# Attention scores from one product with the tokens on the partitions, and maxima and sums of phi taken by halves

## The chip, the cores and the metric

The kernel runs on one core of a Trainium2 chip. The metric is the device time of one execution in microseconds; the time of a version is the median of its runs. A profile is taken by the hardware profiler in one further execution, whose own time stands beside its rows.

Engines are named as the profile names them: PE (matrix products; PEld is its loading of weights, the operand that stays in the array), DVE (vector engine), ACT (scalar engine), POOL, and SP, which here issues DMAs. Each engine works through its own instructions strictly in the order in which they stand in the program.

## The reference

Three parts follow each other; the output of each feeds the next.

```python
# attention: q, k, v [8 batches, 8 heads, 576 tokens, 64], phi [8, 8, 576, 32]
a = exp(phi - phi.max(axis=tokens)); a = a / (a.sum(axis=tokens) + 1e-9)
k_m, v_m = a^T k, a^T v                     # 32 memory rows for each head
scores = (1/8) * q @ k_m^T                  # 576 x 32
attn = softmax(scores over the 32)
x = attn @ v_m                              # [4608 tokens, 512]
# mlp
x = relu(x @ w_in)**2 @ w_out               # 512 -> 2048 -> 512
# experts, top 1 of 8
e = argmax(x @ w_gate); g = softmax(x @ w_gate)[e]
out = g * (relu(x @ w1[e]) @ w2[e])         # 512 -> 1024 -> 512
```

`w_in` and `w_out` arrive as 64-bit floats and are converted on the chip.

## The kernel before

**Stages.** First a start-up, in which `w_in` and `w_out` are loaded in 32 pieces and converted (`conv`: one ACT and three DVE instructions each) and the attention of batch 0 is worked out. Then a main loop over 192 steps: 12 blocks of 384 tokens times 16 pieces of the 2048 hidden columns. Step n makes `h` by six products on PE (`g1`, line 650), three ACT instructions and one DVE instruction make the two halves of `g` from it (658, 660, 661, 662), and three steps later `g2` (line 670) makes nine products of 512 columns into three accumulators. `g` has four buffers. Last come the experts, some 39 tiles of 128 tokens, with weights fetched by expert.

**How attention enters.** The product with `w_in` is folded into the memory rows: for each batch `U = v_m w_in` (`u_steps`, lines 554 and 563 on PE, 569 on ACT, 570 on DVE, eight pieces of 512 columns), and `h` is `U` times the transposed softmax `attnT`. So `g1` of the first step that holds tokens of batch b has to wait for batch b's `attnT` and `U`. Those steps are 16 for batch 1, 32 + 16 = 48 for batch 2, 64 for batch 3, then 96, 112, 144 and 160.

**What one batch's attention does.** `attention(b)` is a generator; the main loop takes a step of it now and then (`R0`, `R1`, `R2` are steps per loop step, `due` and `rel` bound them). Its parts: the maximum of phi (336) over the six tokens j that one partition holds, then over the partitions on POOL, subtraction (343), exponential, the sum over j (350); `s_kv(g)` for two groups g of four heads: the products with phi's weights (366, 374); `s_tr`: their transposes and the block-diagonal `kb` and `vbd`; `s_q`: the transposed queries `qT` of a pair of heads; `s_sc(g)`: scores with the memory rows on the partitions (453), copied by ACT to `sT` (459); `s_soft(g)`: transposes of `sT` back to tokens on partitions (469), then the softmax on DVE and ACT; `s_back(g)`: transposes (492) into `attnT` (496, 497). A phi tile, `e_t`, has one buffer: batch b+1 is loaded when batch b's products have read it.

**Beside it.** `weight_stream` reads the experts' weights through four staging tiles, takes their squares (601, ACT) or maxima (180, DVE), splits them in two halves (628 ACT, 629 DVE) and writes them back. `route` takes each finished block's rows: copies from the accumulators (`x2f`, 706 and 708), scaling into `rec` (723, 724), logits, and a scatter by POOL into a table; the small copy of token numbers into `rec` (791) for the next block has to wait until the scatter of this block has read `rec`.

**What sets the order.** The kernel is recorded in the order of the code, and a scheduler then places the instructions of each engine by its own estimate of when each can run, with priorities around the attention's steps. So an edit moves much more than the lines that it touches. Tiles of the `sd` tag are PSUM banks, three in all, which the attention, `u`, logits and ranks share.

Of the kernel before, what the change touches and what calls it, by code (L numbers as in the profile page):

```python
# [12 lines left out]
F32 = mybir.dt.float32  # L13
# [3 lines left out]
AF = mybir.ActivationFunctionType  # L17
ALU = mybir.AluOpType
AX = mybir.AxisListType
# [4 lines left out]
P = 128  # L24
B, H, S, D, M = 8, 8, 576, 64, 32
DM, DFF, NT, E, F = 512, 2048, 4608, 8, 1024
PS, NJ = 96, 6
# [32 lines left out]
def tile_attention__then__moe__then__moe2(  # L60
# [14 lines left out]
    V, A, G, T, SP = nc.vector, nc.scalar, nc.gpsimd, nc.tensor, nc.sync  # L75
# [5 lines left out]
    ps = ctx_side.enter_context(tc.tile_pool(name="ps", bufs=1, side="right"))  # L81
# [17 lines left out]
    def side_bank(name):  # L99
        return pp.tile([P, 512], F32, tag="sd", name=name, bufs=3)  # L100
# [5 lines left out]
    ident = const([P, P], F32, "ident")  # L106
# [223 lines left out]

    def attention(b):
# [3 lines left out]
        with tc.issue_after(late[b]) if b in late else ExitStack():  # L335
            V.tensor_reduce(
                mx.rearrange("p (h m) -> p h m", h=H), e_t[:PS].rearrange("p h j m -> p h m j"),
                axis=AX.X, op=ALU.max,
            )
# [10 lines left out]
        V.tensor_reduce(  # L350
            es.rearrange("p (h m) -> p h m", h=H), e_t.rearrange("p h j m -> p h m j"),
            axis=AX.X, op=ALU.add,
        )
# [91 lines left out]
        sT, pt = {}, {}  # L445

        def s_sc(g):
            s = ps.tile([P, S], F32, tag="sT", name=f"sT{b}_{g}", bufs=1)
            sT[g] = s
            for hf in range(2):  # L450
                bank = side_bank(f"sc{b}_{g}_{hf}")
                for x in range(2):
                    T.matmul(
                        bank[64 * x:64 * x + 64, 0:288],
                        kbd[g][:, 64 * x:64 * x + 64],
                        qTs[2 * g + x][:, hf * 288:(hf + 1) * 288],
                        start=True, stop=True,
                    )
                A.activation(s[:, hf * 288:(hf + 1) * 288], bank[:, 0:288], AF.Copy)

        def s_soft(g):
# [3 lines left out]
            for hf in range(2):  # L465
                bank = side_bank(f"st{b}_{g}_{hf}")
                for j in range(3):
                    jj = 3 * hf + j
                    T.transpose(
                        bank[:PS, j * P:(j + 1) * P], sT[g][:, jj * PS:(jj + 1) * PS], ident  # L470
                    )
# [42 lines left out]
        s_sc(0)  # L514
# [5 lines left out]
        s_soft(0)  # L520
        yield
# [4 lines left out]
        yield  # L526
        s_sc(1)
# [701 lines left out]
```

## Time and profile before

| | |
|---|---|
| median of 3 runs | 1335.16 us (1334.47 to 1335.77) |
| profiled execution | 1334.69 us, span 1332.6 us |
| PE busy | 1173.5 us, 88% of the span |
| DVE busy | 676.7 us, 51% |
| ACT busy | 661.2 us, 50% |
| granted TensorE clock, mean | 0.958 |
| main loop, first `h` to the last accumulators | about 100 to 866 us |

Shares of busy time are means over stages: the experts keep DVE and ACT nearly idle, while in the main loop all three engines work close together. A busy PE is a union of modelled durations, so short gaps between products don't show in it. The granted clock is 1.00 or 0.50 at a time; a mean between them says how much of a stretch ran at either.

### The profile page before, as it was taken

How to read it: one execution, taken by the hardware profiler on the slowest of the kernel's cores; microseconds unless marked ns; L12 is line 12 of the kernel's file. 1: busy time of each engine (PE TensorE's matmuls, PEld its weight loads, DVE VectorE, ACT ScalarE, POOL GpSimd, SP SyncE). 2: the span in 40 equal slices, each digit the busy share in tenths (PEclk: the TensorE clock that was granted, in tenths of full speed). 3: DMA queues.
4: the chain of work that ended last, by engine and by line, in shares of the span. 5: the costliest groups of instructions: out<-in, count | busy, mean ns of one | idle time of the engine just before them, and what ended most of it. 6: DMA issues, size and time to landing. Idle time of an engine off the chain costs nothing.

```text
span 1332.6 us, 21300 instructions
## 1 busy us (share of the span) xinstructions
PE 1173.5 (88%) x7146; PEld 597.4 (45%) x7146; DVE 676.7 (51%) x1644; ACT 661.2 (50%) x1347; POOL 113.9 (9%) x169
## 2 busy tenths in 40 slices
PE   1538989998988998898999999998998998879896
PEld 1214546444545544455555465543443443334342
DVE  5798987877886885786546543342110111101100
ACT  2467877797875877685666665521111111111111
POOL 2000000101010101000000100013000000000000
PEclk9558999998989999898999999999999999999998
DMA  6957659468749469536040110476558457695762
GB/s 168 261 190 207 189 137 265 158 213 260 216 163 266 154 213 287 159 132 150 24 103 10 40 25 24 126 169 167 97 120 181 104 123 193 151 227 118 151 159 61
DMA packets 264369, 205.23 MB, mean 154 GB/s; under 512 B 209855, under 2 KB 228287, under 8 KB 264256
## 3 DMA queue, kind: packets, MB, share of 16 engines
q1 hardware_dynamic: 257616, 182.67, 53.7%
q0 software_dynamic: 6640, 21.16, 4.6%
q8 instruction: 58, 0.95, 0.3%
q14 instruction: 55, 0.45, 0.1%
HBM read 234.53 MB, written 55.76 MB: 218 GB/s over the span
## 4 chain that ended last, share of the span: by engine, by line
issue 33%; PE 24%; DMA 17%; DVE 13%; ACT 6%; POOL 4%; SPq 2%; POOLq 0%; ACTq 0%; DVEq 0%
PE acc L670 12%; DMA wstage<-in_moe_w_dram 6%; PE h L650 6%; POOL out_dram L92 3%; DMA scr<-rec,sl 2%; DMA e_t<-in_phi_dram 2%; DVE wo L629 2%; ACT wo L628 1%; DMA ws<-wo 1%; PE u L563 1%; DMA raw_ring<-in_moe_w_out_dram 1%; DVE g L662 1%; DMA raw_ring<-in_moe_w_in_dram 1%; ACT wo L601 1%; DVE wm L180 1%
## 5 line engine op out<-in xcount | busy, mean ns | idle before, releaser
L670 PE MATMUL acc<-wo,g 128*128 128x512 f16 x1728 | 421.1, 383 | 16.5 <-DVE g L662 9.9
L670 PEld LDWEIGHTS <-g 128*128 128x128 f16 x1728 | 166.0, 99 | 197.5 <-issue 22.1
L650 PE MATMUL h<-attnT,U 128*128 128x384 f16 (+1 forms) x1536 | 233.5, 290 | 13.8 <-ACT U L569 9.8
L1001 PE MATMUL e<-w2t,gT 128*128 128x512 f16 x936 | 211.5, 381 | 22.3 <-DMA gT<-g 14.6
L974 PE MATMUL e<-w1t,xT 128*128 128x512 f16 x936 | 211.2, 381 | 11.4 <-DMA w1t<-ws 8.0
L986 DVE SCALAR_TENSOR_TENSOR g<-e,g 128x512 f16<-128x512 f32 x78 | 50.3, 686 | 297.5 <-ACT g L985 297.3
L650 PEld LDWEIGHTS <-U 128*128 128x128 f16 x1536 | 140.1, 99 | 104.2 <-issue 26.6
L1001 PEld LDWEIGHTS <-gT 128*128 128x128 f16 x936 | 91.2, 98 | 137.4 <-DMA gT<-g 18.5
L974 PEld LDWEIGHTS <-xT 128*128 128x128 f16 x936 | 91.5, 98 | 124.9 <-issue 13.7
L662 DVE TENSOR_TENSOR g<-r,g 128x384 f16<-128x384 f32 x192 | 105.6, 553 | 78.3 <-ACT r L661 77.8
L658 ACT ACTIVATE r<-h 128x384 f32<-128x384 f32 x192 | 92.6, 485 | 80.7 <-PE h L650 58.7
L985 ACT ACTIVATE g<-e 128x512 f16<-128x512 f32 x78 | 42.3, 594 | 173.6 <-PE e L974 173.6
L1014 ACT ACTIVATE y<-e,fac 128x512 f32<-128x512 f32 x39 | 26.8, 688 | 197.9 <-PE e L1001 190.8
L660 ACT ACTIVATE g<-r 128x384 f16<-128x384 f32 x192 | 99.6, 522 | 8.8 <-PE acc L670 5.2
L661 ACT ACTIVATE r<-r 128x384 f32<-128x384 f32 x192 | 99.5, 521 | 3.9
L629 DVE SCALAR_TENSOR_TENSOR wo<-wstage,wsc,wo 128x1024 f16<-128x1024 f32 x64 | 81.1, 1280 | 21.7 <-ACT wo L628 21.6
L628 ACT ACTIVATE wo<-wstage,wsc 128x1024 f16<-128x1024 f32 x64 | 71.7, 1144 | 25.0 <-DMA ws<-wo 12.6
L92 POOL DMA_INDIRECT out_dram<-y,rt x39 | 37.9, 972 | 377.1 <-ACT y L1014 356.5
L92 POOL DMA_INDIRECT scr<-rec,sl x36 | 37.6, 1043 | 301.8 <-DVE sl L788 66.7
L366 PE MATMUL kvm<-kv,e_t 128*32 128x128 f32 x768 | 28.0, 302 | 28.4 <-ACT e_t L348 27.4
L180 DVE TENSOR_REDUCE wm<-wstage 128x1 f32<-128x1024 f32 x32 | 38.8, 1214 | 14.4 <-DMA wstage<-in_moe_w_dram 14.3
L601 ACT ACTIVATE wo<-wstage 128x1024 bf16<-128x1024 f32 x32 | 33.7, 1054 | 12.3 <-DMA wstage<-in_moe_w_dram 11.0
(240 smaller groups left out, 1088.2 us busy)
## 6 DMA issues: line engine op xcount, KB each, us to landing
w1t<-ws SPq DMA_DIRECT2D x144, 512.0 KB
w2t<-ws SPq DMA_DIRECT2D x144, 512.0 KB
wstage<-in_moe_w_dram SPq DMA_DIRECT2D x64, 512.0 KB
ws<-wo SPq DMA_DIRECT2D x64, 512.0 KB
kv<-in_k_dram SPq DMA_DIRECT2D x16, 576.0 KB
kv<-in_v_dram SPq DMA_DIRECT2D x16, 576.0 KB
q<-in_q_dram SPq DMA_DIRECT2D x64, 144.0 KB
raw_ring<-in_moe_w_in_dram SPq DMA_DIRECT2D x16, 512.0 KB
```

Of the source, the lines that this page charges most:

```text
L92: i = G.indirect_dma_start(out=dst[:, :], out_offset=bass.IndirectOffsetOnAxis(ap=index, axis=0), in_=src, in_offset=None, bounds_check=bo ...
L180: V.tensor_reduce(dst, src, axis=AX.X, op=ALU.max, apply_absolute_value=True)
L628: A.activation(hi, src, AF.Copy, scale=s)
L629: V.scalar_tensor_tensor(lo, src, s, hi, ALU.mult, ALU.subtract)
L650: T.matmul(bank[:, off:off + w], u_t[b][:, g, uh, f * P:(f + 1) * P], attnT[b][:, g, ah, s0:s0 + w], start=(x == 0), stop=(x == len(seq) - 1),
L658: A.activation(r, bank[:, 0:BLK], AF.Relu, scale=2.0 ** -10)
L660: A.activation(g[:, 0], r, AF.Square)
L661: A.activation(r, r, AF.Square)
L662: V.tensor_tensor(g[:, 1], r, g[:, 0], op=ALU.subtract)
L670: T.matmul(a, g[:, gh, tt * P:(tt + 1) * P], wo[:, f, wh, :], start=(f == 0 and x == 0), stop=(f == NF - 1 and x == 2),)
L974: T.matmul(bank[hf], x[:, 4 * xh + c, :].bitcast(F16), w[c][:, wh * F + hf * 512:wh * F + (hf + 1) * 512], start=(c == 0 and xh == 0 and w ...
L1001: T.matmul(a, gT[:, 8 * gh + f, :], w[f // 2][:, o:o + DM], start=(f == 0 and x == 0), stop=(f == 7 and x == 2),)
```

## The change

There are two edits.

The maximum and the sum over the six tokens j of a partition were each one reduction over 1536 elements with stride. They become three elementwise instructions (`over_j`): of two pairs of j into a tile `oj` of 512 elements, with the last pair, and of its two halves into 256.

The scores were made with the memory rows on the partitions, copied to SBUF, and transposed back. Now the transposed queries are the weights and `kb` the moving operand, so that one product gives scores with the tokens on the partitions, in the bank from which the softmax reads. `s_sc`, `sT`, its copies and the transposes of `sT` go. The steps of the generator change with it: `s_soft(0)` stands where `s_sc(0)` stood, and `s_sc(1)`'s step is gone, so that a batch has two steps less.

```diff
+    def over_j(dst, src, op, name):
+        n = src.shape[0]
+        t = ps.tile([P, H, 2, M], F32, tag="oj", name=f"oj{name}", bufs=1)
+        V.tensor_tensor(t[:n], src[:, :, 0:2], src[:, :, 2:4], op=op)
+        V.tensor_tensor(t[:n], t[:n], src[:, :, 4:6], op=op)
+        V.tensor_tensor(dst.rearrange("p (h m) -> p h m", h=H), t[:n, :, 0], t[:n, :, 1], op=op)
...
-            V.tensor_reduce(
-                mx.rearrange("p (h m) -> p h m", h=H), e_t[:PS].rearrange("p h j m -> p h m j"),
-                axis=AX.X, op=ALU.max,
-            )
+            over_j(mx, e_t[:PS], ALU.max, f"mx{b}")
...
-        V.tensor_reduce(
-            es.rearrange("p (h m) -> p h m", h=H), e_t.rearrange("p h j m -> p h m j"),
-            axis=AX.X, op=ALU.add,
-        )
+        over_j(es, e_t, ALU.add, f"es{b}")
...
-        def s_sc(g):
-            s = ps.tile([P, S], F32, tag="sT", name=f"sT{b}_{g}", bufs=1)
-            sT[g] = s
-            for hf in range(2):
-                bank = side_bank(f"sc{b}_{g}_{hf}")
-                for x in range(2):
-                    T.matmul(
-                        bank[64 * x:64 * x + 64, 0:288],
-                        kbd[g][:, 64 * x:64 * x + 64],
-                        qTs[2 * g + x][:, hf * 288:(hf + 1) * 288],
-                        start=True, stop=True,
-                    )
-                A.activation(s[:, hf * 288:(hf + 1) * 288], bank[:, 0:288], AF.Copy)
...
             for hf in range(2):
                 bank = side_bank(f"st{b}_{g}_{hf}")
-                for j in range(3):
-                    jj = 3 * hf + j
-                    T.transpose(
-                        bank[:PS, j * P:(j + 1) * P], sT[g][:, jj * PS:(jj + 1) * PS], ident
-                    )
+                for x in range(2):
+                    for j in range(3):
+                        jj = 3 * hf + j
+                        T.matmul(
+                            bank[:PS, j * P + 64 * x:j * P + 64 * x + 64],
+                            qTs[2 * g + x][:, jj * PS:(jj + 1) * PS],
+                            kbd[g][:, 64 * x:64 * x + 64],
+                            start=True, stop=True,
+                        )
...
-        s_sc(0)
+        s_soft(0)
         yield
         s_tr(1)
         yield
         s_q(2)
-        yield
-        s_soft(0)
         yield
         s_q(3)
         yield "attn"
...
         s_back(0)
-        yield
-        s_sc(1)
         yield
         s_soft(1)
```

Lines of the new version from 348 on have other numbers: 569 is 556 there, 601 is 588, 628 is 615, 658 is 645, 662 is 649, 708 is 695, 496 is 487.

**ACT, around step 16**, where tokens of batch 1 begin. `wm1` is the squares of the weight stream, `x2f0` copies of block 0's rows, `attnT1` and `U1` are batch 1's. Before:

```order
L601 ACTIVATE wo_87,wm1_2447<-wstage_1572 128x1024 x4
L708 ACTIVATE x2f0_0_1633<-acc0_0_949 128x512
L496 ACTIVATE attnT1_1052<-aT1_1_0_1122 128x288
L708 ACTIVATE x2f0_2_1649<-acc0_2_951 128x512
L496 ACTIVATE attnT1_1052<-aT1_1_1_1128 128x288
L569 ACTIVATE U1_1168<-u1_0_0_1169,sb1_1165 128x512
L569 ACTIVATE U1_1168<-u1_0_1_1174,sb1_1165 128x512
```

and now:

```order
L487 ACTIVATE attnT1_1055<-aT1_1_0_1122 128x288
L648 ACTIVATE r15_1493<-r15_1493 128x384
L253 ACTIVATE wo_87<-wo_87,wo_s_761 128x512
L588 ACTIVATE wo_87,wm1_2492<-wstage_1578 128x1024
L556 ACTIVATE U1_1144<-u1_0_0_1145,sb1_1141 128x512
L487 ACTIVATE attnT1_1055<-aT1_1_1_1128 128x288
L588 ACTIVATE wo_87,wm1_2492<-wstage_1578 128x1024
L556 ACTIVATE U1_1144<-u1_0_1_1174,sb1_1141 128x512
```

The last two pieces of `attnT1` stood behind all four squares; now one stands ahead of them and one behind a single square.

**ACT, around step 64**, where tokens of batch 3 begin; `r64` is the first instruction on step 64's `h`. Before, from step 63 on:

```order
L661 ACTIVATE r63_3747<-r63_3747 128x384
L628 ACTIVATE wo16_8_0_5969<-wstage_1572,wsc8_5964 128x1024
L628 ACTIVATE wo16_8_1_6010<-wstage_1572,wsc8_5964 128x1024
L496 ACTIVATE attnT3_3158<-aT3_1_0_3232 128x288
L496 ACTIVATE attnT3_3158<-aT3_1_1_3238 128x288
L569 ACTIVATE U3_3285<-u3_0_0_3286,vts3_3248 128x512
L628 ACTIVATE wo16_8_2_6050<-wstage_1572,wsc8_5964 128x1024
L708 ACTIVATE x2f3_0_3894<-acc3_0_3146 128x512
L601 ACTIVATE wo_87,wm9_6139<-wstage_1572 128x1024
L708 ACTIVATE x2f3_2_3910<-acc3_2_3148 128x512
L628 ACTIVATE wo16_8_3_6106<-wstage_1572,wsc8_5964 128x1024
L569 ACTIVATE U3_3285<-u3_0_1_3295,vts3_3248 128x512
```

and now:

```order
L556 ACTIVATE U3_3177<-u3_0_1_3235,vts3_3162 128x512
L645 ACTIVATE r63_3816<-h63_3809 128x384
L647 ACTIVATE g63_3818<-r63_3816 128x384
L556 ACTIVATE U3_3177<-u3_1_0_3244,vts3_3162 128x512
L648 ACTIVATE r63_3816<-r63_3816 128x384
L556 ACTIVATE U3_3177<-u3_1_1_3281,vts3_3162 128x512
L556 ACTIVATE U3_3177<-u3_2_0_3290,vts3_3162 128x512
L615 ACTIVATE wo16_8_0_6272<-wstage_1578,wsc8_6267 128x1024
L615 ACTIVATE wo16_8_1_6438<-wstage_1578,wsc8_6267 128x1024
L556 ACTIVATE U3_3177<-u3_2_1_3299,vts3_3162 128x512
L645 ACTIVATE r64_3853<-h64_3840 128x384
```

Before, the first piece of `U3` came after step 63's instructions; now six of the eight pieces stand ahead of `r64`.

**DVE, around steps 98 and 99**: `es6` is batch 6's sum of phi, `ojes6` its first piece now, `g98` and `g99` what `g2` waits for. Before:

```order
L662 TENSOR_TENSOR g98_5335<-r98_5333,g98_5335 128x384
L180 TENSOR_REDUCE sm5_5377<-x2f5_2_5361 128x1
L481 TENSOR_REDUCE st5_0_5301<-pt5_0_5300 96x12
L736 TENSOR_SCALAR sm6_6193<-sm6_6193,wo_s_761 128x3
L482 TENSOR_SCALAR st5_0_5301<-st5_0_5301 96x12
L350 TENSOR_REDUCE es6_5804<-e_t_95 128x256
L180 TENSOR_REDUCE wm14_8448<-wstage_1572 128x1
L180 TENSOR_REDUCE sm5_5377<-x2f5_1_5353 128x1
L662 TENSOR_TENSOR g99_5404<-r99_5402,g99_5404 128x384
```

and now:

```order
L649 TENSOR_TENSOR g98_5378<-r98_5376,g98_5378 128x384
L180 TENSOR_REDUCE sm5_5447<-x2f5_1_5396 128x1
L466 TENSOR_TENSOR pt5_1_5339<-st5_1_0_5341,st5_1_5340 96x384
L334 TENSOR_TENSOR ojes6_5667<-e_t_95 128x512
L180 TENSOR_REDUCE wm14_8713<-wstage_1578 128x1
L616 SCALAR_TENSOR_TENSOR wo16_13_3_8680<-wstage_1578,wsc13_8576,wo16_13_3_8680 128x2x512
L180 TENSOR_REDUCE sm5_5447<-x2f5_2_5404 128x1
L466 TENSOR_TENSOR pt5_1_5339<-st5_1_1_5351,st5_1_5340 96x384
L649 TENSOR_TENSOR g99_5474<-r99_5472,g99_5474 128x384
```

Only the first piece of the sum stands between the two now, but other work has come in beside it.

## Rows read from the trace of the kernel before

**Rows 1.** Busy time by stretch of the span, in us, then granted clock, DMA.

```profile
core 0: us, PE busy (x) PEld busy (x) DVE busy (x) ACT busy (x) POOL busy (x), PEclk, DMA share, GB/s
...
62.00:96.00 34.00, 14.84 (x46) 4.74 (x46) 31.36 (x65) 18.94 (x38) 2.91 (x2) 0.54 0.64 191
...
370.00:412.00 42.00, 33.65 (x318) 19.74 (x316) 30.27 (x84) 28.82 (x59) 4.38 (x5) 0.88 0.68 214
...
630.00:866.00 236.00, 235.42 (x1576) 129.57 (x1575) 113.14 (x346) 143.18 (x312) 16.45 (x17) 1.00 0.19 49
```

**Rows 2.** The groups by line and shape: count, busy us, mean ns of one, idle before.

```profile
L662 DVE TENSOR_TENSOR g<-r,g 128x384 f16<-128x384 f32 x192 | 105.6, 553 | 78.3 <-ACT r L661 77.8
...
L350 DVE TENSOR_REDUCE es<-e_t 128x256 f32<-128x1536 f32 x8 | 22.6, 2830 | 0.0
L336 DVE TENSOR_REDUCE mx<-e_t 96x256 f32<-96x1536 f32 x8 | 22.5, 2811 | 7.7 <-DMA e_t<-in_phi_dram 7.7
...
L343 DVE TENSOR_TENSOR e_t<-e_t,mxa 96x1536 f32<-96x1536 f32 x8 | 14.0, 1752 | 3.1 <-POOL mxa L341 3.1
...
L459 ACT ACTIVATE sT<-sc 128x288 f32<-128x288 f32 x32 | 12.6, 401 | 10.2 <-PE sc L453 10.2
```

**Rows 3.** PE in order of time: start, us, one half of the scores, their transposes.

```profile
650.00 0.71 PE L453 MATMUL sc<-qT,kb 128*64 128x288 f32 x4
650.64 1.15 PE L650 MATMUL h<-attnT,U 128*128 128x384 f16 x6
...
652.49 0.49 PE L469 MATMUL st<-ident,sT 128*96 128x128 f32 x3
652.82 0.38 PE L670 MATMUL acc<-wo,g 128*128 128x512 f16 x1
```

**Rows 4.** PE in order of time, the product of one column.

```profile
684.99 0.38 PE L374 MATMUL kvm<-cols,es 128*128 128x1 f32 x2
685.23 0.59 PE L670 MATMUL acc<-wo,g 128*128 128x512 f16 x2
```

**Rows 5.** ACT in order of time at step 16, then PE.

```profile
170.94 1.06 ACT L601 ACTIVATE wo<-wstage 128x1024 bf16<-128x1024 f32 x1 [1.07 <-DVE wo L254]
...
177.07 0.71 ACT L569 ACTIVATE U<-u,sb 128x512 f16<-128x512 f32 x1
...
177.87 1.42 PE L554 MATMUL u<-w_in_sb,vbd 128*64 128x512 f32 x4 [3.04 <-DVE wt L175]
```

**Rows 6.** ACT and PE in order of time at step 64.

```profile
383.28 1.25 ACT L569 ACTIVATE U<-u,vts 128x512 f16<-128x512 f32 x2
...
384.01 0.82 PE L650 MATMUL h<-attnT,U 128*128 128x192 f16 x4 [2.92 <-ACT U L569]
```

**Rows 7.** Busy time and granted clock of the two stretches around these waits.

```profile
174.00:182.00 8.00, 4.96 (x18) 1.39 (x16) 6.08 (x22) 6.43 (x13) 0.35 (x1) 0.79 0.00 0
...
381.00:390.00 9.00, 5.19 (x26) 2.31 (x26) 7.55 (x23) 7.98 (x16) 0.00 (x0) 0.63 0.83 290
```

**Rows 8.** DVE in order of time around steps 98 and 99.

```profile
536.64 1.29 DVE L629 SCALAR_TENSOR_TENSOR wo<-wstage,wsc,wo 128x1024 f16<-128x1024 f32 x1
...
538.30 0.69 DVE L180 TENSOR_REDUCE sm<-x2f 128x1 f32<-128x512 f32 x1
...
539.56 2.81 DVE L350 TENSOR_REDUCE es<-e_t 128x256 f32<-128x1536 f32 x1
542.27 1.22 DVE L180 TENSOR_REDUCE wm<-wstage 128x1 f32<-128x1024 f32 x1
...
543.99 0.56 DVE L662 TENSOR_TENSOR g<-r,g 128x384 f16<-128x384 f32 x1
```

**Rows 9.** Who waited for whom in the main loop: us in total, times, longest.

```profile
PE kvT L394 <- DVE kvn L385: 4.8, 2, 4.5
...
DVE rec L791 <- DMA scr<-rec,sl: 37.4, 22, 6.4
```

More of the change, by code (lines that the diff above doesn't have):

```diff
@@ L443, in s_q @@
             qTs[pr] = qT
-        sT, pt = {}, {}
-        def s_sc(g):
-            s = ps.tile([P, S], F32, tag="sT", name=f"sT{b}_{g}", bufs=1)
-            sT[g] = s
-            for hf in range(2):
-                bank = side_bank(f"sc{b}_{g}_{hf}")
-                for x in range(2):
-                    T.matmul(
-                        bank[64 * x:64 * x + 64, 0:288],
-                        kbd[g][:, 64 * x:64 * x + 64],
-                        qTs[2 * g + x][:, hf * 288:(hf + 1) * 288],
-                        start=True, stop=True,
-                    )
-                A.activation(s[:, hf * 288:(hf + 1) * 288], bank[:, 0:288], AF.Copy)
+        pt = {}
         def s_soft(g):
```

## The prediction

> **What bounds the kernel now.** I read busy time by stretch first. The page's means (PE 88%, DVE and ACT half) hide three different limits. In the start-up, from 62 to 96 us, DVE is busy 31.36 of 34 us [rows 1]: the conversions, batch 0's softmax and batch 1's first phi work stand end to end on it. At the end of the main loop, from 630 to 866 us, PE is busy 235.42 of 236 us while DVE and ACT have much room [rows 1]: there only work on PE counts. Between them PE should be as full, and is not: from 370 to 412 us it is busy 33.65 of 42 us, and its clock is granted at 0.88 [rows 1]. That is where time can come from without PE's work shrinking.
>
> So I went on to the list of waits and to the order of time around the long ones. Two of them are the attention coming late. Around step 16, ACT starts a square of the weight stream at 170.94 and does four in a row; batch 1's last copies and the first piece of its `U` wait behind them until 177.07, and PE stands 3.04 us at a `u` product, which needs a bank that these copies free [rows 5]. Around step 64, PE waits 2.92 us for the first pieces of `U` of batch 3, evicted at 383.28 [rows 6]. Each wait costs more than itself: around them, once PE has stood, the granted clock falls from 2.4 to 1.2 GHz for a while, and its mean is 0.79 over 8 us and 0.63 over 9 us [rows 7], that is 8 x 0.21 = 1.7 us and 9 x 0.37 = 3.3 us of lost PE time. Other long waits have another cause: DVE's copies of token numbers into `rec` wait for the scatter, 37.4 us in 22 times and 6.4 us at the longest, and PE then waits up to 4.5 us for a `kvn` that is queued behind such a copy [rows 9].
>
> **The change, part by part.** The sum is made against the profiled execution, 1334.69 us, which is 0.5 us under the median of 1335.16.
>
> *Maxima and sums.* The strided reductions take 2.81 and 2.83 us each, eight of either [rows 2]. Elementwise float instructions take 553 ns for 384 elements and 1752 ns for 1536 [rows 2], so (1752 - 553) / 1152 = 1.041 ns an element; 512 elements are then 0.69 us, 256 are 0.42 us, and the three together 1.79 us. Each of 16 gets 1.03 us shorter, 16.5 us of DVE in all. In the start-up, where DVE is the limit, I count the two of batch 1 that stand at and in the full stretch: -2 us. The two of batch 0 stand where DVE still waits for loads: 0; counted too, they would make it -4, and if the loads set the start-up's end it is 0. In the main loop DVE's time lies beside PE's, and counts only where a wait is for DVE. One such place is around step 99: after `g98` DVE works on until 543.99 before it comes to `g99`, 5.69 us from 538.30 on, with a sum of 2.81 us in it [rows 8]. But the new order puts seven instructions there: 0.69 + 0.55 + 0.69 + 1.22 + 1.29 + 0.69 + 0.55 = 5.68 us, by [rows 2, 8] (the first piece of the sum is the third of them). So nothing is gained there: 0.
>
> *Scores.* Off PE go, for each group of heads, two times 0.64 us of scores and two times 0.33 us of transposes [rows 3]: 1.94 us. What comes is 12 products of 64 columns with 96 columns of weights. A float product stands as two records in the trace (four for two products in [rows 3]), so 24 records, each with weights of its own. No row has this shape. The lower bound is the moving side alone: three transposes of 128 columns take 0.33 us [rows 3], 0.11 each, so 0.055 for 64 columns; 24 of them are 1.32 us, 0.62 less than before. A bound from the weights is the product of one column: two records with 128 columns of weights take 0.24 us [rows 4], 0.12 each, so 0.09 for 96 columns; 24 are 2.16 us, 0.22 more than before. If weights and columns followed each other without overlap it would be 0.145 a record, 3.48 us, 1.54 more. I take 0.085, near the weights' row, since the first load in that row follows no product of its own kind that could hide it: 2.04 us, 0.1 more. Batch 0 stands in the start-up, where PE has room (14.84 of 34 us [rows 1]); the other 14 groups stand in the main loop: +1.5 us, with ends at -8.7 and +21.6.
>
> *ACT.* 32 copies of 0.40 us go [rows 2], 12.8 us, and with each a passage from PE to ACT and back that the transposes waited for. ACT is no limit over a long stretch, and PE works on other products meanwhile: 0 by itself. If that cover is gone, it shows in the next term.
>
> *Attention earlier.* The batch loses two steps and two such passages, and the order shows what follows. At step 16 one copy of `attnT1` now stands ahead of the squares, and one square, not four, stands ahead of the first piece of `U1` and of the other copy. Of 3.04 + 1.7 = 4.7 us [rows 5, 7] I give back one square, 1.06 us [rows 5]: -3.5 us. It is 0 if the accumulators' copies, which now come later, become what PE waits for. At step 64 six pieces of `U3` stand ahead of the first instruction on `h64`, where before the second piece stood behind two copies, a square and the weight stream: the wait and its clock, 2.92 + 3.3 [rows 6, 7], go: -6 us, at least -3 if only the wait goes. What is late next there is the weight stream, two of whose ACT instructions now stand behind six pieces of `U3`; its end is not waited for before the experts, and SP's loads for it come later with it.
>
> *Waits for the scatter.* The copies into `rec` have less ahead of them in some blocks. Counted on DVE between the last write of a block's record and the token copy for the next one, block 0 goes from 15 to 9 instructions, block 5 from 29 to 16, block 8 from 14 to 8; blocks 2 and 3 gain, from 20 to 27 and from 14 to 22. Behind such a copy queue `g` and `kvn`, and PE after them. After 630 us PE has cover enough. Of the rest, I count half of one wait of the longest kind, 4.5 us on PE [rows 9]: +2 us (0 to +4.5).
>
> Sum: -2 + 0 + 1.5 + 0 - 3.5 - 6 + 2 = **-8 us**, 1326.7 for a profiled execution, **1327 us** for the median. The ends don't fall together; between -14 and -2 is what I expect of this case: 1321 to 1333 us.
>
> **The rivals.**
>
> *The waits only move.* Every instruction in the main loop has a new place. The two waits may go and others of the same kind come, at steps 16 and 112, say, where batches 1 and 5 begin. For it: the waits of the list are spread over many pairs, and step 99 shows a long reduction replaced by as much other work [rows 8]. Against it: 12.8 us of ACT and 16.5 us of DVE are really gone. The gains of 9.5 us at steps 16 and 64 are then given back, but not the start-up: 1334.7 - 2 + 1.5, with a few us to either side, 1332 to 1338.
>
> *More goes than these two.* If the smaller waits for DVE and ACT shrink as the attention's work does, and the products come out at their lower end, up to 15 us more is gained: 1312 to 1321.
>
> *The weights are not hidden.* Then each record costs 0.145 us, and +1.5 becomes +21.6: -8 + 20 = +12, **1347 us**, slower. It decides from 24 x - 1.94 = 0.68 us on (9.5 / 14), that is from 0.109 us a record. For it: the one-column row shows 0.12 for a load of 128 columns with hardly anything to stream [rows 4]. Against it: the three transposes follow each other every 0.11 us though each loads 96 columns of weights [rows 3], so loads do run beside products there.
>
> The Trainium skill, in "TensorE: Matmul & The Clock Gate" (section "Part 3: Packing small matmuls — row/col tiling"), says that a weight load overlaps products in flight only when it goes to another group of rows. The new products all use the full height, so by that page this rival holds, with the 1347 us above. The transposes of [rows 3] use the full height as well and follow at the pace of their columns, so this trace speaks against the rule as it stands; no run here yet has a stream with as few columns as the new one.
>
> *A queue behind the scatter.* If two or all three of the blocks that lose cover make PE wait 4.5 us and let the clock fall, 1.7 us, that is 12 to 19 us in place of 2: +2 to +9, 1337 to 1344 us. For it: such a wait of PE is in the list twice already. Against it: four buffers of `g` cover most of them now (22 waits on DVE, but two on PE for `kvn` [rows 9]).
>
> **How the numbers follow.** The forecast has a chance of 0.55, waits that only move 0.17, the larger gain 0.10, the queue behind the scatter 0.11, weights not hidden 0.07. About 0.2%, 2.7 us, is what a measurement of this kernel can tell from no change. Faster by more: the forecast and the larger gain, 0.65. Slower by more: the last two, 0.18. The rest, 0.17, is the same. The range of 8 in 10 holds the forecast, the case without movement, half of the larger gain and the start of the scatter's case: 1317 to 1339 us.
>
> **What the changed kernel's profile would show.** The products of the scores: 24 records in about 2.0 us, 0.085 apart; 0.06 speaks for the lower end, 0.14 for unhidden weights. The three DVE pieces: 0.69, 0.69 and 0.42 us. The wait of `u` around step 16 under 1.5 us, no wait for `U` at step 64, and no half clock at these two. The first `h` about 2 us earlier. The expert stage as long as before. I am wrong if the main loop's full part, where PE is the limit, gets longer, if new half-clock stretches take the place of those two, or if DVE's waits for the scatter grow past 45 us and PE's with them.

## The result and the profile after

| | before | changed |
|---|---|---|
| median | 1334.82 us, 4 runs (1334.13 to 1335.77) | 1314.14 us, 4 runs (1307.0 to 1319.59) |
| profiled execution | 1334.69 us, span 1332.6 us | 1313.53 us, span 1311.5 us |
| first `h` | 100.4 us | 102.9 us |
| main loop, first `h` to the experts' first product | 773.4 us | 744.0 us |
| from there to the end | 458.8 us | 464.6 us |
| half clock within the main loop | 40.5 us | 26.2 us |

The ratio is 0.9845 (95% interval 0.9803 to 0.9886): faster by 20.7 us, where I forecast 8. Against the terms of the sum, the main loop gave 29.4 us where I had 6 (0 + 1.5 - 3.5 - 6 + 2), the start-up took 2.5 us where I had it give 2, and the rest took 5.8 us where I had nothing.

First the stretches of [rows 1] and of [rows 7] in the changed kernel (62 to 96 and 370 to 412 us as there, the others moved to where the same work stands now): stretch, busy time of each engine, granted clock, DMA.

```profile
core 0: us, PE busy (x) PEld busy (x) DVE busy (x) ACT busy (x) POOL busy (x), PEclk, DMA share, GB/s
62.00:96.00 34.00, 13.46 (x51) 6.64 (x53) 29.45 (x59) 15.61 (x29) 1.43 (x1) 0.50 0.64 188
102.00:847.00 745.00, 719.15 (x5192) 409.79 (x5193) 513.17 (x1312) 534.20 (x1103) 62.97 (x64) 0.98 0.56 156
160.00:168.00 8.00, 8.00 (x47) 4.15 (x46) 6.94 (x15) 6.58 (x13) 0.00 (x0) 1.00 0.00 0
370.00:412.00 42.00, 38.77 (x396) 25.62 (x393) 32.34 (x96) 34.13 (x73) 5.85 (x6) 1.00 1.00 269
365.00:374.00 9.00, 9.00 (x65) 4.33 (x64) 7.69 (x15) 6.19 (x11) 0.36 (x1) 1.00 0.17 60
630.00:839.00 209.00, 208.53 (x1424) 116.25 (x1422) 100.28 (x308) 127.26 (x274) 13.29 (x14) 1.00 0.19 48
```

The stretches around steps 16 (160 to 168 us) and 64 (365 to 374 us) are now full, at full clock, and PE waits for nothing from 158 to 178 us or from 360 to 381 us: both waits that I had counted are gone, with their half clock. From 370 to 412 us PE is busy 38.77 us, not 33.65 [rows 1]. The start-up's stretch of DVE is less full (29.45 of 34, before 31.36), and the first `h` comes no earlier all the same.

Then the new instructions in the list of groups, and the start of one group of scores on PE in order of time.

```profile
L334 DVE TENSOR_TENSOR ojmx<-e_t 96x512 f32<-96x512 f32 x8 | 5.5, 684 | 13.8 <-DMA e_t<-in_phi_dram 13.8
...
L335 DVE TENSOR_TENSOR ojes<-ojes,e_t 128x512 f32<-128x512 f32 x8 | 5.4, 680 | 0.0
L336 DVE TENSOR_TENSOR es<-ojes 128x256 f32<-128x256 f32 x8 | 3.3, 413 | 0.0
```

```profile
673.22 0.87 PE L457 MATMUL st<-kb,qT 128*96 128x64 f32 x8
673.93 0.38 PE L657 MATMUL acc<-wo,g 128*128 128x512 f16 x1
674.15 0.30 PE L457 MATMUL st<-kb,qT 128*96 128x64 f32 x2
674.29 0.38 PE L657 MATMUL acc<-wo,g 128*128 128x512 f16 x1
```

The pieces take 0.684, 0.680 and 0.413 us; [rows 2] had given 0.69, 0.69 and 0.42. Eight records of the new products take 0.71 us until the next product starts, 0.089 each; over the 294 neighbouring pairs of them at full clock the median is 0.085. Both costs came out as worked out.

Last the waits of PE from 105 to 845 us: us in total, times, longest.

```profile
PE lg L787 <- ACT qT L441: 4.3, 1, 4.3
PE st L457 <- DVE attnT L488: 3.5, 1, 3.5
PE lg L787 <- DMA xTb<-rec: 3.0, 3, 2.1
PE aT L483 <- DVE vts L177: 2.8, 1, 2.8
PE kvm L367 <- DMA kv<-in_v_dram: 2.2, 1, 2.2
...
PE acc L657 <- DVE g L649: 0.5, 1, 0.5
```

Two rows of the same view of the kernel before:

```profile
PE acc L670 <- DVE g L662: 9.9, 9, 3.1
...
PE acc L670 <- DVE x2f L706: 4.2, 1, 4.2
```

All rows of this view add up to 24.5 us (45.4 before). Gone are not only the waits of steps 16 and 64 but nearly all of the accumulators' products for `g`, that for `x2f`, most of `kvT` for `kvn` [rows 9] and most others; some new ones of 2 to 4 us have come. 20.9 us of waits and (40.5 - 26.2) / 2 = 7.2 us of half clock are 28 of the main loop's 29.4 us.

### The profile page after: what moved, and what is told of

It is laid out like the page before. It is cut to its first block, busy times and chain, and to the rows that moved or that the text cites. A ratio compares the mean times of both kernels' runs of the same rounds, so it can differ in the third digit from the quotient of the medians.

```text
span 1311.5 us, 21652 instructions
## 1 busy us (share of the span) xinstructions
PE 1172.5 (89%) x7306; PEld 615.5 (47%) x7306; DVE 659.2 (50%) x1676; ACT 649.6 (50%) x1315; POOL 120.9 (9%) x169
## 4 chain that ended last, share of the span: by engine, by line
PE 33%; issue 33%; DMA 15%; DVE 9%; ACT 5%; POOL 3%; SPq 0%; POOLq 0%; ACTq 0%; DVEq 0%
PE acc L657 17%; PE h L637 9%; DMA wstage<-in_moe_w_dram 5%; DMA ws<-wo 3%; POOL out_dram L92 3%; DMA raw_ring<-in_moe_w_in_dram 2%; DVE wo L616 2%; DMA e_t<-in_phi_dram 2%; ACT wo L615 1%; DMA xTb<-rec 1%; PE e L961 1%; PE st L457 1%; PE u L541 1%; PE u L550 1%; PE kvm L367 1%
## 5 line engine op out<-in xcount | busy, mean ns | idle before, releaser
L988 PE MATMUL e<-w2t,gT 128*128 128x512 f16 x936 | 217.3, 389 | 25.1 <-DMA gT<-g 21.6
L649 DVE TENSOR_TENSOR g<-r,g 128x384 f16<-128x384 f32 x192 | 106.1, 555 | 95.4 <-ACT r L648 94.5
L1001 ACT ACTIVATE y<-e,fac 128x512 f32<-128x512 f32 x39 | 26.8, 688 | 207.7 <-PE e L988 199.2
L648 ACT ACTIVATE r<-r 128x384 f32<-128x384 f32 x192 | 99.8, 520 | 3.6
L457 PE MATMUL st<-kb,qT 128*96 128x64 f32 x384 | 42.0, 266 | 3.5 <-DVE attnT L488 3.5
```

The costliest lines, as they stand in the source:

```text
L457: T.matmul(bank[:PS, j * P + 64 * x:j * P + 64 * x + 64], qTs[2 * g + x][:, jj * PS:(jj + 1) * PS], kbd[g][:, 64 * x:64 * x + 64], start=T ...
L648: A.activation(r, r, AF.Square)
L649: V.tensor_tensor(g[:, 1], r, g[:, 0], op=ALU.subtract)
L988: T.matmul(a, gT[:, 8 * gh + f, :], w[f // 2][:, o:o + DM], start=(f == 0 and x == 0), stop=(f == 7 and x == 2),)
```

## The experiments

Three theories stood at the start. First, mine: the scores' edit removes a passage from PE to ACT and back and two steps of each batch, and that makes the gain. Second: the halves make it, since no instruction on DVE is long any more. Third: any other order of the work moves the time by as much. All ratios are to the kernel before, timed in between.

### Parts of the change alone

Scores' edit without the halves:

```diff
-            over_j(mx, e_t[:PS], ALU.max, f"mx{b}")
+            V.tensor_reduce(mx..., e_t[:PS]..., axis=AX.X, op=ALU.max)
...
-        over_j(es, e_t, ALU.add, f"es{b}")
+        V.tensor_reduce(es..., e_t..., axis=AX.X, op=ALU.add)
```

> The changed kernel with the two reductions of phi back as single instructions; the scores' products and the shorter list of steps stay. First theory (mine): the gain of 20.7 us comes from the scores' edit, which takes a passage from TensorE to ScalarE and back out of every group of heads and two steps out of every image, and each wait of TensorE that goes takes a stretch of half clock with it: 1312 to 1322 us. Second theory: the long instructions on VectorE held up what the main loop waits for, and the halves made most of the gain: 1328 to 1336 us. Third theory: nothing particular was removed; any other order of the work moves the time by this much: anywhere from 1310 to 1340 us, and the effects of the parts don't add up.

Halves without the scores' edit (the diff's `over_j` in the kernel before; this differs from it):

```diff
-        t = ps.tile([P, H, 2, M], F32, tag="oj", name=f"oj{name}", bufs=1)
+        w = ps.tile([P, S], F32, tag="sT", name=f"oj{name}", bufs=1)
+        t = w[:, 0:H * 2 * M].rearrange("p (h j m) -> p h j m", h=H, j=2)
```

> The kernel before with only the maxima and sums of phi taken by halves (the intermediate tile shares the buffer of the copied scores, since there is no room for another). First theory: 1329 to 1335 us, a gain of 0 to 5 us. Second theory: 1314 to 1321 us. Third theory: anywhere from 1310 to 1340 us.

Two steps less, with the old products, copies and transposes:

```diff
         s_sc(0)
+        s_soft(0)
         yield
...
-        s_soft(0)
-        yield
...
         s_sc(1)
-        yield
         s_soft(1)
```

> The kernel before with its products, its copies on ScalarE and its transposes, but with each group's scores and softmax in one step, at the place that the changed kernel has, so that each image has two steps less and the attention ends earlier. First theory: the passage over ScalarE now stands inside one step and TensorE waits for it twice per group, so the earlier end is paid for: 1328 to 1345 us. A variant of it, in which the two steps alone make the gain: 1312 to 1322 us. Second theory: no difference to the kernel before, 1333 to 1337 us. Third theory: anywhere from 1310 to 1340 us.

The changed kernel with the old number of steps:

```diff
-        s_soft(0)
         yield
...
+        s_soft(0)
+        yield
...
+        yield
         s_soft(1)
```

> The changed kernel with the softmax of each group at the place that it had before and an empty step where the scores' step was, so that each image has as many steps as before; products and halves as in the changed kernel. First theory: most of the gain stays, since the passage over ScalarE is gone and its waits with it: 1316 to 1325 us; if the two steps alone made it: 1330 to 1337 us. Second theory: 1314 to 1321 us. Third theory: anywhere from 1310 to 1340 us.

| kernel | median, us | ratio, 95% | first `h` | main loop |
|---|---|---|---|---|
| scores' edit alone | 1330.24 | 0.9973 (0.9948 to 0.9999) | 104.2 | 760.1 |
| halves alone | 1325.93 | 0.9958 (0.9932 to 0.9983) | 96.3 | 766.1 |
| two steps less alone | 1326.08 | 0.9951 (0.9930 to 0.9972) | 101.4 | 761.6 |
| changed, old steps | 1331.86 | 1.0007 (0.9984 to 1.0030) | 106.1 | 760.7 |

Neither of the first two theories holds: no part brings more than 7 us, and the last kernel has both edits and gains nothing. Nor do the parts add up: 0.0027 for the scores' edit and 0.0042 for the halves are 0.007, where the two together brought 0.0155 in the first runs. The 35 runs of the kernel before beside these lay between 1326.3 and 1342.84 us, with a median of 1332.21, so single runs of one kernel are some 10 us apart, and a few runs are no measure of a few us.

### The same kernels again, and in other orders

The changed kernel as it is:

> The changed kernel, unaltered, once more. The four kernels with only a part of the change gave ratios of 0.9973, 0.9958, 0.9951 and 1.0007, none of them anywhere near 0.9845, and single runs of a kernel lie some 10 us apart. If the parts add up (products and steps 13 us of the main loop together, halves 7 us, as the traces of those four read): a ratio of 0.983 to 0.988 again, so 1310 to 1317 us, and a second trace whose waits stand at the same steps as in the first. If the first four runs were lucky ones: 0.990 to 0.996, with other waits in the second trace.

The kernel before as it is (its expectation was written after the runs with 2.4 to 2.7 below):

> The kernel before, unaltered, for a second trace. Two traces of the changed kernel differ in the duration of only one step of the main loop by more than 1.5 us. If the same holds here, its main loop takes 771 to 776 us from the first h to the last accumulator (773.2 in the first trace), with 20 to 28 us of idle time for g, and the 29 us between the two kernels' main loops belong to the two orders; if not, some of it was luck of the one trace.

The changed kernel again gave 1316.21 us, ratio 0.9869 (0.9834 to 0.9905); the gain is no luck of the first runs. In its second trace one step of 191 differs by more than 1.5 us from the first trace (5.15 for 3.52 us), and the main loop takes 743.9 us (744.0). The kernel before, in its second trace: three steps differ, and the main loop takes 774.9 us (773.4), with these waits of PE from 105 to 845 us, nearly those of the first trace.

```profile
PE acc L670 <- DVE g L662: 10.3, 11, 3.1
PE qTp L435 <- ACT qT L440: 5.7, 4, 3.7
PE kvT L394 <- DVE kvn L385: 4.9, 2, 4.7
PE acc L670 <- DVE x2f L706: 4.5, 1, 4.5
PE lg L800 <- DVE pt L475: 2.8, 2, 1.9
PE h L650 <- ACT r L658: 2.6, 3, 1.6
PE u L554 <- DVE wt L175: 2.6, 1, 2.6
```

So the waits of the main loop belong to the program, and the runs of one kernel differ elsewhere: the first `h` stands at 102.9 and 106.7 us in the two traces of the changed kernel, and what follows the main loop takes 458.8 and 455.1 us in those of the kernel before.

Next, one number of the plan in both kernels, steps of the attention for each step of the main loop. No operation comes or goes; the attention's steps only move against the main loop.

```diff
-R2 = 2.5
+R2 = 2.6
```

> The changed kernel with one number of the plan changed: 2.6 in place of 2.5 steps of the attention for each step of the main loop while one is under way. Not one operation is added or taken away; the steps of the attention only move by a step or so against the main loop. If the change took something particular away: within 4 us of the changed kernel. If any order of the work has its own set of waits (third theory) and the changed kernel drew a good one: 1318 to 1332 us.

> The kernel before with the same number of the plan changed, 2.6 in place of 2.5. If the waits of the kernel before belong to its passage over ScalarE and its long reductions: within 4 us of the kernel before. Third theory: it moves by 5 to 15 us, and the direction can't be told ahead.

And with 2.4 and 2.7 in place of 2.6:

> The kernel before with 2.4 in place of 2.5 steps of the attention for each step of the main loop. Two theories are left. A: the change itself is worth some 5 us of the time (its products save ScalarE its copies, and fewer products of the main loop wait for g), and the rest of the 17 to 20 us belongs to the order that the changed kernel happens to have; then this kernel lies at 1325 to 1336 us, and the mean of the kernels before at 2.4 to 2.7 lies 3 to 8 us above the mean of the changed ones. B: the change is worth 15 us or more, and 2.6 was a bad number for it: 1329 to 1337 us here.

> The changed kernel with 2.4 in place of 2.5. Theory A: 1318 to 1331 us. Theory B: 1311 to 1319 us.

> The kernel before with 2.7 in place of 2.5. Theory A: 1325 to 1336 us. Theory B: 1329 to 1337 us.

> The changed kernel with 2.7 in place of 2.5. Theory A: 1318 to 1331 us. Theory B: 1311 to 1319 us.

| `R2` | before: median, ratio | main loop | changed: median, ratio | main loop | ratios apart |
|---|---|---|---|---|---|
| 2.4 | 1339.50, 1.0050 (1.0033 to 1.0067) | 774.4 | 1329.70, 0.9983 (0.9965 to 1.0001) | 765.4 | -0.0067 |
| 2.5 | the reference, 1 | 773.4, 774.9 | 1316.21, 0.9869 (0.9834 to 0.9905) | 744.0, 743.9 | -0.0131 |
| 2.6 | 1328.35, 0.9967 (0.9944 to 0.9989) | 762.3 | 1327.87, 0.9958 (0.9935 to 0.9981) | 759.2 | -0.0009 |
| 2.7 | 1329.06, 0.9983 (0.9967 to 0.9999) | 771.8 | 1321.18, 0.9918 (0.9889 to 0.9948) | 751.8 | -0.0065 |

The mean of the last column is -0.0068, that is 9 us of 1332. The four differ from each other by a standard deviation of 0.005 (7 us), so their mean is uncertain by about as much as it is large, 0.008 at 95%. Theory A, written before the runs at 2.4 and 2.7, had a gap of 3 to 8 us between the two means; theory B had 15 us or more. Of the four times that each gave for the runs at 2.4 and 2.7, A missed one (1339.50 for 1325 to 1336) and B three (that one, and 1329.70 and 1321.18 for 1311 to 1319). So A fits better, but the uncertainty of the mean, some 11 us, doesn't exclude 15. In the traces, and with the mean of the two traces at 2.5, the four changed kernels start the first `h` 4.8 us later (104.6 for 99.8), pass the main loop in 15.6 us less (755.1 for 770.7), and need the same 460.5 us from there on.

PE's idle time in the main loop stands out of the orders more clearly than the time does. Summed over all its waits from the first `h` to the experts' first product, at 2.4 to 2.7, it is 48.8, 46.4 (two traces), 42.9 and 48.3 us before, and 34.3, 24.8 (two traces), 33.2 and 31.5 us in the changed kernels: 15.6 us less in the mean, 7.8 to 23.5 at 95%. The two waits that the prediction counted belong to this in every order. In the five traces of the kernel before, PE stands 2.6 to 3.1 us before `u` of step 16 and 1.9 to 5.9 us for `U` of step 64; in the five of the changed kernel it has no wait from 160 to 190 us, and at most 0.3 us for `U` of step 64. The wait of step 64 stays with the halves alone (2.7 us) and is 0.4 us with the scores' edit alone or two steps less alone, 0.6 us in the changed kernel with the old steps. At step 16, though, that last kernel has `u` wait 3.4 us again (around 177 to 180 us).

The halves at equal work for DVE:

```diff
         V.tensor_tensor(t[:n], src[:, :, 0:2], src[:, :, 2:4], op=op)
+        V.tensor_tensor(t[:n], src[:, :, 0:2], src[:, :, 2:4], op=op)
         V.tensor_tensor(t[:n], t[:n], src[:, :, 4:6], op=op)
         V.tensor_tensor(dst..., t[:n, :, 0], t[:n, :, 1], op=op)
+        V.tensor_tensor(dst..., t[:n, :, 0], t[:n, :, 1], op=op)
```

> The changed kernel in which the first and the last piece of every maximum and every sum of phi are issued twice with the same result, so that a maximum or a sum takes VectorE as long as the single reduction did (0.68 x 3 + 0.41 x 2 = 2.87 us by the rows after, 2.83 us before), but in five short instructions. If the halves help since no instruction on VectorE is longer than 0.7 us: the time of the changed kernel within 4 us. If they help since they are less work for VectorE: the time of the kernel with the products and steps alone, 13 to 17 us above the changed kernel. Third theory: 1318 to 1332 us.

1329.17 us, ratio 0.9979 (0.9955 to 1.0004). It tells nothing: the changed kernel lies there too when only `R2` is moved. Its main loop is short (749.1 us) and its first `h` late (111.0 us), which fits a start-up in which DVE is the limit [rows 1].

### Why the accumulators' products wait less for `g`

One sum separates kernels with the new products from those without in every trace so far: the idle time before line 670 (657 in the changed kernel), loads and products together, that ended with `g`. For the kernel before (second trace), the changed kernel and the changed kernel at 2.6, from 105 to 870 us:

```profile
its engine sat idle before it (us, times) until:
  DVE g L662: 26.8, 24
```

```profile
its engine sat idle before it (us, times) until:
  issue: 12.4, 32
  DVE g L649: 2.5, 5
```

```profile
its engine sat idle before it (us, times) until:
  issue: 13.9, 46
  DVE g L649: 12.7, 7
```

Without the new products this idle time is 14.3 to 26.8 us (seven traces), with them 1.6 to 12.7 us (eight). But the view adds up the idle time of PE and of PEld, which run side by side, so the sum isn't time that passed. In the whole trace of the kernel before, the two rows are

```profile
L670 PE MATMUL acc<-wo,g 128*128 128x512 f16 x1728 | 421.1, 383 | 16.5 <-DVE g L662 9.9 <-DVE x2f L706 4.2 <-ACT x2f L708 1.5
...
L670 PEld LDWEIGHTS <-g 128*128 128x128 f16 x1728 | 166.0, 99 | 197.5 <-issue 22.1 <-DVE g L662 15.4 <-ACT g L660 1.1
```

PE's own idle time for `g` is 5.0 to 10.3 us without the new products and 0.3 to 5.5 us with them in the same traces. It is shorter with them in each of the four orders (1.3 for 5.0, 0.4 for 10.1, 5.5 for 8.5 and 1.0 for 8.5 us), but the two ranges overlap. Five runs looked for the reason; their expectations speak of the sum. ScalarE's copies put back:

```diff
+                for x in range(2):
+                    jk = ps.tile([P, 192], F16, tag="jk", name=f"jk{b}_{g}_{hf}_{x}", bufs=1)
+                    A.activation(jk[:PS], bank[:PS, 192 * x:192 * x + 192], AF.Copy)
                 src = bank[:PS, 0:3 * P].rearrange("p (x m) -> p x m", m=M)
```

> The changed kernel with copies on ScalarE put back beside the scores: two copies of 96 x 192 scores from each bank into a tile that nobody reads, so eight per image and some 0.3 us each by the row of the old copies (0.40 us for 288 columns), one and a half times the work that the change took from ScalarE; nobody waits for them. In fourteen traces the accumulators' products in the main loop idle 14.3 to 25.2 us for g, 15 to 23 times, where the scores are copied and transposed, and 1.6 to 12.7 us, 3 to 7 times, where the new products stand. If ScalarE's saved work is the reason: 14 us or more here, 12 times or more, and a time of 1325 to 1336 us. If the missing passage (a product on TensorE that waits for ScalarE, and VectorE behind it) is the reason: at most 13 us and 8 times; the time itself may lie anywhere from 1314 to 1332 us, since the order of the work moves.

> The same copies, at 2.7 in place of 2.5 steps of the attention for each step of the main loop, so that the reading doesn't hang on one order of the work. If ScalarE's saved work is the reason: 14 us or more for g; if the passage is: at most 13 us and 8 times. Time against the changed kernel at 2.7 (1321 us): 5 to 12 us more by the first, within 6 us by the second.

The old copies on DVE:

```diff
-                A.activation(s[:, hf * 288:(hf + 1) * 288], bank[:, 0:288], AF.Copy)
+                V.tensor_copy(s[:, hf * 288:(hf + 1) * 288], bank[:, 0:288])
```

> The kernel before with its copies of the scores on VectorE in place of ScalarE: the passage from TensorE to another engine and back stays, ScalarE is spared its 0.40 us four times per image, and VectorE gets them. If ScalarE's saved work is the reason for the fewer waits for g: below 13 us and 8 times or fewer. If the passage is: 14 us or more, 12 times or more, and 1330 to 1342 us, since VectorE has more to do ahead of g.

A passage in front of the new products:

```diff
+                few = qTs[2 * g][:, 3 * hf * PS:3 * hf * PS + 8]
+                T.matmul(bank[:, 400:408], ident, few, start=True, stop=True)
+                A.activation(few, bank[:, 400:408], AF.Copy)
                 for x in range(2):
```

> The changed kernel with a passage from TensorE to ScalarE and back in front of each half of the scores, with hardly any work in it: a product with the identity gives eight columns of qT again, ScalarE copies them back to their place (128 x 8), and the half's products read them. The copies of the scores without a passage left the idle time of the accumulators' products for g at 10.5 us and 3.7 us (12 and 6 times), and VectorE's copies with the passage at 19.2 us (10 times). If the passage is the reason: 14 us or more here, 12 times or more, and a time of 1322 to 1336 us. If it is neither the passage nor ScalarE's work but something else that came with the new products (where they stand in TensorE's order, what they leave beside them): at most 13 us, 8 times, and 1314 to 1330 us.

> The same at 2.7 in place of 2.5 steps of the attention for each step of the main loop, where the changed kernel waits 3.9 us for g (6 times) and takes 1321 us. If the passage is the reason: 14 us or more for g and 1324 to 1336 us; if not: at most 13 us and a time of 1314 to 1328 us.

The same view of the kernel with copies back on ACT at 2.5, and of that with the passage at 2.7:

```profile
its engine sat idle before it (us, times) until:
  DVE g L652: 10.5, 12
```

```profile
its engine sat idle before it (us, times) until:
  issue: 15.4, 33
  DVE g L652: 5.8, 7
```

| kernel | idle for `g`, us (times) | of PE alone | all idle time of PE in the main loop | median, us | ratio, 95% | main loop |
|---|---|---|---|---|---|---|
| changed, copies back on ACT | 10.5 (12) | 3.8 | 32.4 | 1321.05 | 0.9905 (0.9874 to 0.9935) | 749.5 |
| the same at 2.7 | 3.7 (6) | 1.2 | 31.2 | 1315.73 | 0.9877 (0.9850 to 0.9904) | 750.6 |
| before, copies on DVE | 19.2 (10) | 9.8 | 56.9 | 1352.77 | 1.0139 (1.0109 to 1.0169) | 786.4 |
| changed, with a passage | 4.0 (7) | 1.3 | 40.4 | 1332.02 | 1.0010 (0.9989 to 1.0031) | 766.5 |
| the same at 2.7 | 5.8 (7) | 2.0 | 35.7 | 1327.19 | 0.9963 (0.9940 to 0.9985) | 760.9 |

One execution of the kernel with copies on DVE took 3042 us and is left out of its ratio. ScalarE's saved work is not the reason: with one and a half times that work given back, the idle time stays on the side of the new products, if near its edge in one order, and at 2.7 the time is no longer than that of the changed kernel. The passage isn't it either: 4.0 and 5.8 us. These two kernels are slower than the changed ones in the same order, by 16 and 6 us, but the passage isn't as light as I wrote: its products are 64 records with 128 columns of weights, and two such records took 0.24 us [rows 4], so 28 pairs in the main loop are, as an estimate, 6.7 us of PE. And PE idles more in their main loops, 40.4 us for 24.8 and 35.7 for 31.5, though hardly for `g`; 6.2 and 8.3 us of it, before the transposes of `q`, have no releaser in the profile. So a passage may well be part of the 15.6 us by which PE idles less; two orders don't tell. Why `g` is waited for less stays open: the sum is at most 12.7 us in all twelve traces that have the new products and at least 14.3 us in the eight that don't, and nothing that I put back or moved took a kernel to the other side. A run that holds PE's order fixed and changes the products alone wasn't tried.

## Why the prediction was wrong

**Where it was right.** The products' price came out at 0.085 us a record, as taken, and with it the rival of unhidden weights (0.145) is out. (14 groups at 0.10 us more are 1.4 us, where I wrote 1.5.) By the Trainium skill's rule that I weighed there ("TensorE: Matmul & The Clock Gate", "Part 3: Packing small matmuls — row/col tiling") a load would not overlap products of the same rows; these full-height records follow each other at 0.085 to 0.089 us, faster than the estimate of 0.145 for load and columns one after the other, so the measurement decides against the rule here. The three pieces on DVE cost what [rows 2] gave. The waits at steps 16 and 64 went, with their half clock; of 4.7 + 6.2 = 10.9 us that the two places held I had counted 9.5. They went in all four orders, so this part of the mechanism held.

**The step that failed** is the size of the term *attention earlier*. It took the two waits that belong to late attention by name, -9.5 us with their half clock, for all that the change could take from PE's waits. Without the clock they are 6.0 us (3.04 + 2.92) of 20.9 that went: 9.4 us (9.9 to 0.5) were waits for `g`, nine of them and only one over 3 us, which I had left in the rival in which more goes; another 4.2 us was one for `x2f`. In the mean of the four orders the two waits are 6 of the 15.6 us that go, and those for `g` another 6 (8.0 to 2.0). The list of waits had those for `g` at its top, and a sum over kinds rather than over long single waits would have put more chance there than 0.10. That the halves or ACT's lighter load shortened them, as that rival had it, isn't shown: the halves alone leave PE 9.7 us of idle time for `g`, and ACT's load is ruled out above.

The one wait over 3 us is that of step 99, where I had counted 0 because as much work stands between `g98` and `g99` on DVE as before. The count was right, but the wait went all the same. Before, on PE:

```profile
544.60 4.02 PE L670 MATMUL acc<-wo,g 128*128 128x512 f16 x9 [3.06 <-DVE g L662]
```

and now, on DVE and PE:

```profile
523.06 0.67 DVE L180 TENSOR_REDUCE sm<-x2f 128x1 f32<-128x512 f32 x1
...
528.10 0.54 DVE L649 TENSOR_TENSOR g<-r,g 128x384 f16<-128x384 f32 x1
```

```profile
529.88 3.40 PE L657 MATMUL acc<-wo,g 128*128 128x512 f16 x15
```

DVE still works 5.0 us before it comes to `g99` (5.7 before), but PE comes to the next products only after `g99` is done. It had itself been held up, by 3.5 us for `attnT` until 515.4 us and half clock until 521.6; that this is why it no longer waits is argued, not shown. Steps 96 to 103 take 35.2 us, before 38.0. So the work ahead of `g` on DVE doesn't give the wait; when PE needs it counts as much.

**What stood behind it.** The forecast treated the order as fixed but for the places that I had compared. The scheduler makes a new order out of any edit, and that alone moves the time: by 11 us between the kernels before at 2.4 and at 2.6, by 13.5 us between the changed kernels at 2.4 and 2.5. Over the four orders the change is worth 9 us, uncertain by as much. That this is near the 8 us of the sum is an agreement of totals alone: in the traces the main loop gave 15.6 us where the sum had 6, and the first `h` came 4.8 us later where it had 2 us earlier. The same operations in the one order that was timed give 17 (0.9869) to 21 us (0.9845). I had the order's part as a rival only in the direction of no gain. A range for one order should have been wider downward by those 10 us, and the 2.7 us that I took a measurement to tell from no change says nothing of other orders.

**The smaller terms.** *Maxima and sums*: -2 us in the start-up. With the halves alone the first `h` comes 4.1 us earlier (96.3 for 100.4), my outer end. But with the new products it comes at 102.4 to 111.0 us in all twelve traces, without them at 96.3 to 101.4, but for the one that gave DVE more work (109.5). So the scores' edit costs some 5 us where I had it free since PE has room. What the first `h` waits for is ACT's eviction of `U` in the kernel before and after alike. In the 10 us ahead of it ACT is busy 9.58 us in the changed kernel (92.9 to 102.9 us) and 7.81 before (90.4 to 100.4), in both with the conversion of `w_out`; what put more of it there I haven't tried. *Waits for the scatter*: +2 us. DVE's waits for it fell from 37.4 us to 24.1 us, the longest from 6.4 to 3.3, though I had counted less cover in three blocks; PE's wait for `kvn` fell from 4.8 to 1.0 us. But this is largely the order's: at 2.4, 2.6 and 2.7 the waits for the scatter are 30.3 to 36.6 us in the changed kernels and 32.9 to 41.5 before, and PE waits 0.3 to 5.3 us in all for `kvn` in the former and 0.3 to 1.4 in the latter. Instructions counted between two writes don't tell how long they take to come up. *The end*: the 5.8 us more after the main loop are no part of the change: over the four pairs the difference is nothing, and from one trace to another that part takes 455 to 468 us.

## What to carry to other kernels

Where a scheduler lays out the work anew after each edit, time a change in several orders of equal work (move a number of the plan that adds no operation, in both versions) before you put its gain down to an operation; here that alone was worth as much as the edit. A profile prices the operations well (the new products and the three pieces came out within a few per cent), but which waits remain is a property of the whole order: sum the waits of the limiting engine by kind, and widen the range by what edits without an operation move. To keep a lucky order is fine, as long as the next edit isn't blamed for losing it.

## What was not expected

Two executions of one program repeat the main loop nearly step for step: 743.9 and 744.0 us, 773.4 and 774.9 us, with one and three steps of 191 apart by more than 1.5 us, while whole runs of one kernel lie 7 to 18 us apart. So one trace was enough here to read the waits of the loop, but not the start-up or the experts.

A granted clock of 1.00 can mean that nothing was recorded. In the kernel with the scores' edit alone the view of stretches gives 1.00 from 62 to 96 us:

```profile
62.00:96.00 34.00, 13.31 (x52) 6.87 (x52) 31.59 (x61) 15.19 (x26) 1.50 (x1) 1.00 0.66 198
```

But the same four records of `u` take 1.98 us there just before the first `h` and 1.08 us soon behind it:

```profile
97.08 1.98 PE L540 MATMUL u<-w_in_sb,vbd 128*64 128x512 f32 x4 [0.78 <-DVE w_in_red L281]
...
109.13 1.08 PE L540 MATMUL u<-w_in_sb,vbd 128*64 128x512 f32 x4
```

So PE ran at half clock in the start-up as in the changed kernel (0.50 above); the first record of its clock stands at 108.7 us. A mean clock of 0.98 beside 0.95 for another run says nothing here before durations are compared.
